# Slot work of three batches joined in the last two head pairs of a chunk-select attention and soft-MoE kernel

## The chip, the core and the metric

The kernel runs on one core of one Trainium2 chip. The metric is device time in microseconds (us), the median of several executions; lower is better. Engines: PE is TensorE, DVE is VectorE, ACT is ScalarE, POOL is GpSimd (it also issues the loads), SP issues the stores.

## The reference, cut to what matters

```python
# attention: B=4, H=8, S=768, D=64; chunks of 32 keys, the 6 best per query by a bound
scores = where(mask(top_chunks, causal), q @ k.T / sqrt(D), -1e9)
x = softmax(scores) @ v                      # -> [3072, 512], all batches in one table
# soft MoE: 8 experts of 4 slots, so 32 slots; F = 1024
logits = x @ phi                             # [3072, 32]
d = softmax of logits down the 3072 rows     # one softmax over all four batches
slot_input = d.T @ x                         # [32, 512]
h = relu(slot_input[e] @ w1[e]);  slot_out[e] = h @ w2[e]
c = softmax of logits along the 32 slots
out = c @ slot_out                           # [3072, 512]
```

The softmax d runs over all rows of all batches, so no slot input is final before the last batch's attention is done.

## The kernel before, in words

The work is cut into 16 pairs of heads, four pairs to a batch (pairs 0 to 3 are batch 0, 12 to 15 batch 3). One hand-written loop (L466 to L550) runs over i from -2 to 15, and iteration i, called pair i here, holds a software pipeline: k and q of pair i + 4 are loaded, k and q of pair i + 2 are transposed on PE and copied by ACT (L181, L190), DVE makes chunk bounds and the split of q (L199 to L216), pair i + 1 gets its chunk selection (ubound, select), pair i gets its scores in six groups (scores, L270 and L280, each group into one of two PSUM buffers) with exponents on ACT (expo, L293) and a causal select on POOL (L295), pair i - 1 gets its product with v (pv, L314, one PSUM buffer), and pair i - 2 is normalised into x (normalise, L326 and L327) and transposed into xT (x_transposes, evac_x). The order in the loop is the order on every engine: each engine takes its instructions strictly as written, and a manual schedule reorders nothing. Matmul results other than scores and pv go through two PSUM buffers (pool p_tp).

The slot work of a batch follows the batch's last pair, two and three iterations later. For batch 0 (last pair 3) it stands in pairs 5 and 6, for batch 1 in pairs 9 and 10, for batch 2 in pairs 13 and 14. At the end of the first of the two, moe_logits (L356, 24 matmuls) and moe_copy (L364 copies the logits, L365 takes each lane's max). In the second, spread over the pair: moe_max (L371 transposes the maxima), moe_bound (L378), moe_exp (a broadcast of the max by PE, the running max m_run, the shifted logits ld, ACT's exponent d_sb at L397 and, from batch 1 on, the rescaling of the sums si_acc), moe_comb (row max L410, difference L412, ACT's exponents into c_pad, L415), moe_dispatch (L426, 30 matmuls that weight x by d and add up the weights, then into si_acc) and moe_ct (L440 transposes c_pad, L443 copies it to cT_all). This is an online softmax: each batch rescales what was summed before. Batch 3 is done behind the loop (L556 to L622), with a few extra matmuls (keep, L570), then come the experts (L650 to L716) and the output (L719 to L745).

The 16 weight blocks (1 MB each in SBUF, w1 of experts 0 to 7, then w2) are loaded by POOL through one software queue, with the loads of k, q and v (192 KB each per pair). Block 0 is issued at the start; the dictionary wplan gives one block to each pair from -1 on except 0 and 1. Blocks 0 to 13 have places of their own (EARLY = 14). Blocks 14 and 15 lie where the input and bound buffers were (pools inp and tpu) and are issued at the start of pairs 14 and 15. The expert code reads blocks 12 to 15 first in experts_out(0, [1], ...), at L711 (the matmul is L694).

Of the kernel before, what the change touches and what calls it, by code (L numbers as in the profile page):

```python
# [46 lines left out]
def kernel(  # L47
# [19 lines left out]
    EARLY = 14  # L67
# [251 lines left out]
    def normalise(i, t0=0, t1=NQT, at=None):  # L319
        b, j = divmod(i, NPB)  # L320
        at = st.pop(("at", i)) if at is None else at
        at = at[:, :, :(t1 - t0) * (D + 1)].rearrange("p h (t d) -> p h t d", t=t1 - t0)
        if j == 0:
            st["x", b] = xp.tile([P, NQT, H, D], BF16, name="x_sb", tag="x_sb")
        inv = tp2.tile([P, 2, NQT, 1], F32, name="inv", tag="inv")[:, :, t0:t1]
        nc.vector.reciprocal(inv, at[:, :, :, D:D + 1])  # L326
        nc.vector.tensor_tensor(  # L327
            st["x", b][:, t0:t1, 2 * j:2 * j + 2, :].rearrange("p t h d -> p h t d"),
            at[:, :, :, :D], inv.broadcast_to([P, 2, t1 - t0, D]), op=ALU.mult,
        )  # L330
# [30 lines left out]
    def moe_copy(b):  # L361
        lg = small.tile([P, NQT, NS], F32, name="lg", tag="lg")
        pm = small.tile([P, NS], F32, name="pm", tag="pm")
        nc.vector.tensor_copy(lg, st.pop(("lgps", b)))  # L364
        nc.vector.tensor_reduce(pm, lg.rearrange("p t s -> p s t"), axis=AX.X, op=ALU.max)  # L365
        st["lg", b], st["pm", b] = lg, pm

    def moe_max(b):
# [2 lines left out]
        nc.tensor.matmul(pmT, lhsT=st.pop(("pm", b)), rhs=identf, is_transpose=True)  # L371
        st["pmT", b] = pmT

    def moe_bound(b):

        pmT = st.pop(("pmT", b))
        mb = small.tile([NS, 1], F32, name="mb", tag="mb")
        nc.vector.tensor_reduce(mb, pmT, axis=AX.X, op=ALU.max)  # L378
        st["mb", b] = mb

    def moe_exp(b):
        lg = st["lg", b]
        bc = p_tp.tile([P, NS], F32, name="bc_ps", tag="tp")
        nc.tensor.matmul(
            bc, lhsT=st.pop(("mb", b)).broadcast_to([NS, P]), rhs=identf[:NS, :NS], start=True, stop=True,
        )
        m_new, m_old = m_run[b % 2], m_run[(b + 1) % 2]
        if b == 0:
            nc.vector.tensor_copy(m_new, bc)
        else:  # L390
            nc.vector.tensor_tensor(m_new, m_old, bc, op=ALU.max)
        ld = small.tile([P, NQT, NS], F32, name="ld", tag="ld")
        nc.vector.tensor_tensor(
            ld, lg, m_new.rearrange("p (o s) -> p o s", o=1).broadcast_to([P, NQT, NS]), op=ALU.subtract,
        )
        d_sb = small.tile([P, NQT, NS], BF16, name="d_sb", tag="d_sb")
        nc.scalar.activation(d_sb, ld, func=ACT.Exp)  # L397
        st["d", b] = d_sb
        if b > 0:

            dm = small.tile([P, 1, NS], F32, name="dm", tag="dm")
            nc.vector.tensor_tensor(dm[:, 0, :], m_old, m_new, op=ALU.subtract)
            nc.scalar.activation(dm, dm, func=ACT.Exp)
            nc.vector.tensor_tensor(si_acc, si_acc, dm.broadcast_to([P, NDG + 1, NS]), op=ALU.mult)

    def moe_comb(b):

        lg = st.pop(("lg", b))
        rm = small.tile([P, NQT, 1], F32, name="rm", tag="rm")
        nc.vector.tensor_reduce(rm, lg, axis=AX.X, op=ALU.max)  # L410
        lc = small.tile([P, NQT, NS], F32, name="lc", tag="lc")
        nc.vector.tensor_tensor(lc, lg, rm.broadcast_to([P, NQT, NS]), op=ALU.subtract)  # L412

        for g in range(2):
            nc.scalar.activation(  # L415
                c_pad[:, :, :, g * SPE:(g + 1) * SPE],
                lc[:, :, g * 16:(g + 1) * 16].rearrange("p t (j s) -> p t j s", j=4), func=ACT.Exp,
            )

    def moe_dispatch(b):  # L420
        d_sb = st.pop(("d", b))
        x = st.pop(("x", b)).rearrange("p t h d -> p t (h d)").rearrange("p t (a c x) -> p t a x c", a=NDG // 2, x=2)
        si = p_tp.tile([P, NDG + 1, NS], F32, name="si_ps", tag="tp")
        for dg in range(NDG + 1):
            for t in range(NQT):
                nc.tensor.matmul(  # L426
                    si[:, dg, :], lhsT=x[:, t, dg // 2, dg % 2, :] if dg < NDG else ones_sq,
                    rhs=d_sb[:, t, :], start=(t == 0), stop=(t == NQT - 1),
                )
        if b == 0:  # L430
            nc.vector.tensor_copy(si_acc, si)
        elif b < B - 1:
            nc.vector.tensor_tensor(si_acc, si_acc, si, op=ALU.add)
        else:
            st["si"] = si

    def moe_ct(b):
        ps = p_tp.tile([P, NQT, P], BF16, name="cT_ps", tag="tp")
        for t in range(NQT):
            nc.tensor.matmul(  # L440
                ps[:, t, :], lhsT=c_pad[:, t].rearrange("p j s -> p (j s)"), rhs=ident, is_transpose=True,
            )
        nc.vector.tensor_copy(cT_all[:, b * NQT:(b + 1) * NQT, :], ps)  # L443
# [12 lines left out]
    for i in (0, 1):
        wplan[i] = 0
    nw = 1

    def weights(i):  # L460
        nonlocal nw
        for _ in range(wplan.get(i, 0)):
            load_w(nw)
            nw += 1

    for i in range(-2, NPAIR):  # L466
        if i >= EARLY:
            wt = ctx.enter_context(tc.tile_pool(name=f"wt{i}", bufs=1))
            w_sb.append(wt.tile([P, NFG * Dm], BF16, name=f"w_sb{i}"))
            weights(i)  # L470
# [5 lines left out]
        moe(moe_max, i - 3)  # L476
# [56 lines left out]
        moe(moe_dispatch, i - 3)  # L533
# [10 lines left out]
        moe(moe_ct, i - 3)  # L544
        moe(moe_logits, i - 2)
        moe(moe_copy, i - 2)
        if i == LAST - 2:
            l_ctx.close()
        if i == LAST - 1:
            u_ctx.close()  # L550

    pads = ctx.enter_context(tc.tile_pool(name="pads", bufs=1))
    siT_pad = pads.tile([P, NDG, E, CH], BF16, name="siT_pad")
    hT_pad = pads.tile([P, NFG, E, CH], BF16, name="hT_pad")
# [52 lines left out]
    st["d", BL] = d_sb  # L607
# [168 lines left out]
```

## Time and profile before

| | us |
|---|---|
| measured time, median of 3 | 173.73 (173.69 to 173.76) |
| span of the profiled execution | 172.0 |
| from one kT copy to the next, pair 8 to 9 | 6.86 |
| pairs 5 to 6, 6 to 7, 7 to 8 | 8.14, 8.75, 7.15 |
| pairs 9 to 10, 10 to 11 | 8.06, 9.56 |
| last exponent of the loop (L293) starts | 134.13 |
| first matmul of the experts (L654) | 141.80 |
| first store issued | 153.58 |

The profiled execution's own time is its span, 172.0 us from the first to the last instruction; the measured time of a run is 1.7 us more. Shares of the span: PE busy 80%, DVE 73%, ACT 71%, POOL 58%. Times in the text are us from the span's start. A line such as L293 is a line of the kernel; a group of instructions is told by its line, engine, and the tiles that it writes and reads.

### The profile page before, as it was taken

What the parts mean: (1) busy time and instruction counts of PE and PEld (TensorE: products, weight loads), DVE (VectorE), ACT (ScalarE), POOL (GpSimd) and SP (SyncE); (2) the same over time, 40 slices, a digit from 0 to 9 for tenths busy, and PEclk for the clock granted to TensorE, in tenths of its full rate; (3) what the DMA queues carried; (4) which work ended last, traced back from release to release, by engine and by line L of the source; (5) the groups of instructions that cost most, each with busy time, mean ns of one, the idle gap of its engine ahead of it and who ended that gap; (6) DMA issues with size and microseconds to landing.
All of it is one profiled execution on the core that took longest, in us unless ns stands there. A gap on an engine that the chain in (4) does not pass through costs nothing.

```text
span 172.0 us, 6181 instructions
## 1 busy us (share of the span) xinstructions
PE 137.7 (80%) x2574; PEld 99.3 (58%) x2575; DVE 126.0 (73%) x429; ACT 122.2 (71%) x163; POOL 99.7 (58%) x192
## 2 busy tenths in 40 slices
PE   0458988999999789999988899999697989896310
PEld 0345465776767658766675676676565854774200
DVE  3468768999999988999997989999843652156530
ACT  2355999999999679899977799998567621265430
POOL 7977759789878666889774678558253710000000
PEclk9999999999999999999999999999999999999955
DMA  3999999999999999999999999999999950019995
GB/s 46 169 145 188 184 213 187 130 159 210 171 203 194 210 198 206 198 205 201 204 202 200 206 197 209 195 211 198 202 210 213 215 107 0 4 37 402 403 406 221
DMA packets 40460, 32.94 MB, mean 191 GB/s; under 512 B 26352, under 2 KB 34544, under 8 KB 40432
## 3 DMA queue, kind: packets, MB, share of 16 engines
q0 software_dynamic: 38416, 26.25, 103.2%
q1 hardware_dynamic: 2016, 6.29, 9.3%
q8 instruction: 20, 0.33, 0.7%
q14 instruction: 8, 0.07, 0.1%
HBM read 52.49 MB, written 6.29 MB: 342 GB/s over the span
## 4 chain that ended last, share of the span: by engine, by line
PE 37%; ACT 27%; DVE 17%; DMA 8%; issue 7%; POOL 0%; ACTq 0%; DVEq 0%; POOLq 0%
ACT e_sb L293 20%; PE sc_ps L270 7%; DMA out_dram<-o_sb 6%; PE tr_ps L181 5%; PE at_ps L314 5%; PE sc_ps L280 4%; DVE x_sb L327 3%; PE h_ps L654 2%; PE so_ps L694 2%; DVE qpn L216 2%; PE ub_ps L229 2%; DMA k_in<-in_k_dram 2%; ACT kT L190 2%; DVE mm L199 2%; DVE mm L205 2%
## 5 line engine op out<-in xcount | busy, mean ns | idle before, releaser
L293 ACT ACTIVATE e_sb<-sc_ps 128x768 bf16<-128x768 f32 (+1 forms) x96 | 82.7, 927 | 7.0 <-PE sc_ps L280 6.5
L295 POOL TENSOR_SCALAR_AFFINE_SELECT e_sb<-e_sb 128x256 bf16<-128x256 bf16 x96 | 39.2, 415 | 25.6 <-ACT e_sb L293 25.3
L270 PE MATMUL sc_ps<-qT,kT 64*128 64x384 bf16 (+3 forms) x288 | 40.2, 297 | 6.6 <-ACT e_sb L293 6.5
L280 PE MATMUL sc_ps<-nsT,smask 64*128 64x384 bf16 (+2 forms) x320 | 38.7, 281 | 0.0
L314 PE MATMUL at_ps<-v_t,e_sb 128*128 128x65 bf16 x672 | 29.8, 194 | 1.8 <-DVE x_sb L327 1.6
L270 PEld LDWEIGHTS <-kT 64*128 64x128 bf16 x288 | 17.3, 95 | 18.3 <-issue 13.2
L314 PEld LDWEIGHTS <-e_sb 128*128 128x128 bf16 x672 | 25.2, 98 | 4.2 <-issue 1.5
L241 DVE MAX8 mx<-ub_ps 128x8 f32<-128x8 f32 (+1 forms) x192 | 17.0, 162 | 3.4 <-POOL e_sb L295 1.9
L280 PEld LDWEIGHTS <-smask 64*128 64x128 bf16 x320 | 16.7, 96 | 3.6 <-issue 0.6
L190 ACT COPY kT<-tr_ps 128x768 bf16<-128x768 bf16 x16 | 12.8, 798 | 8.2 <-PE tr_ps L181 7.1
L199 DVE TENSOR_REDUCE mm<-kT 128x24 bf16<-128x768 bf16 x16 | 15.1, 944 | 4.1 <-ACT kT L190 4.0
L134 POOL DMA_DIRECT2D v_t<-in_v_dram x16 | 16.6, 1041 | 2.0 <-PE ns_ps L252 1.3
L327 DVE TENSOR_TENSOR x_sb<-at_ps,inv 128x768 bf16<-128x768 f32 (+1 forms) x17 | 15.5, 910 | 0.6
L205 DVE TENSOR_REDUCE mm<-kT 128x24 bf16<-128x768 bf16 x16 | 15.1, 943 | 0.0
L190 ACT COPY qT<-tr_ps 128x768 bf16<-128x768 bf16 x16 | 12.9, 805 | 2.1 <-PE tr_ps L181 2.1
L181 PE MATMUL tr_ps<-ident,k_in 128*64 128x128 bf16 x192 | 9.4, 240 | 5.6 <-DMA k_in<-in_k_dram 4.8
L129 POOL DMA_DIRECT2D k_in<-in_k_dram x16 | 11.7, 729 | 1.5 <-POOLq L760 0.8
L740 ACT ACTIVATE o_sb<-o_ps,cinv 128x512 f32<-128x512 f32 x12 | 8.1, 686 | 5.6 <-DMA out_dram<-o_sb 4.3
L129 POOL DMA_DIRECT2D q_in<-in_q_dram x16 | 11.5, 720 | 0.0
L216 DVE TENSOR_SCALAR qpn<-qT 128x768 bf16<-128x768 bf16 x16 | 11.5, 716 | 0.0
L122 POOL DMA_DIRECT2D w_sb<-in_moe_w_dram x16 | 11.3, 708 | 0.0
L738 DVE TENSOR_SCALAR o_sb<-o_ps,cinv 128x512 f32<-128x512 f32 x11 | 8.0, 748 | 4.3 <-DMA out_dram<-o_sb 3.1
(116 smaller groups left out, 195.5 us busy)
## 6 DMA issues: line engine op xcount, KB each, us to landing
w_sb<-in_moe_w_dram POOLq DMA_DIRECT2D x16, 1024.0 KB, 13.4
out_dram<-o_sb SPq DMA_DIRECT2D x10, 512.0 KB, 5.4
k_in<-in_k_dram POOLq DMA_DIRECT2D x16, 192.0 KB, 9.6
q_in<-in_q_dram POOLq DMA_DIRECT2D x16, 192.0 KB, 9.6
v_t<-in_v_dram POOLq DMA_DIRECT2D x16, 192.0 KB, 10.1
out_dram<-o_sb SPq DMA_DIRECT2D x4, 256.0 KB, 3.3
phi_sb<-in_moe_phi_dram POOLq DMA_DIRECT2D x1, 32.0 KB, 8.8
```

Source lines behind the costliest of these rows:

```text
L129: nc.gpsimd.dma_start(out=t, in_=src.rearrange("h (p g) d -> p h (g d)", p=P))
L181: nc.tensor.matmul(ps[h * 64:(h + 1) * 64, g, :], lhsT=src[:, h, g * D:(g + 1) * D], rhs=ident, is_transpose=True,)
L190: nc.scalar.copy(t.rearrange("d (p g) -> d p g", g=NQT), st.pop((nm + "ps", i)).rearrange("d g p -> d p g"),)
L199: nc.vector.tensor_reduce(mm[:, 0, 0, :], kT, axis=AX.X, op=ALU.min)
L205: nc.vector.tensor_reduce(mm[:, 1, 0, :], kT, axis=AX.X, op=ALU.max)
L241: nc.vector.max(mx[:, a, :], ub[:, a, :max(8, 4 * t + 4)])
L270: nc.tensor.matmul(ps[:, h, c:c + w], lhsT=kT[r, kg * P:(kg + 1) * P], rhs=qT[r, qs], start=True, stop=False,)
L280: nc.tensor.matmul(ps[:, h, c + (f - t0) * P:c + (l - t0) * P], lhsT=smask[r, x, kg].rearrange("p a b -> p (a b)"), rhs=nsT[r, (f - x * NJ ...
L293: nc.scalar.activation(e[:, :, :w], st.pop(("scps", i, g))[:, :, :w], func=ACT.Exp, scale=scale)
L295: nc.gpsimd.affine_select(out=e[:, :, :P], in_=e[:, :, :P], compare_op=ALU.is_ge, fill=0.0, base=0, pattern=[[0, 2], [1, P]], channel_mult ...
L314: nc.tensor.matmul(o, lhsT=st["e", i, g][:, h, c:c + P], rhs=v_t[i % NV][:, h, kg, :], start=(kg == 0), stop=(kg == t),)
L327: nc.vector.tensor_tensor(st["x", b][:, t0:t1, 2 * j:2 * j + 2, :].rearrange("p t h d -> p h t d"), at[:, :, :, :D], inv.broadcast_to([P, ...
```

## The change

The logits of batches 0 to 2 are only copied (into lg_all). Their softmax, dispatch and combine weights are done once for all 18 row tiles: the max over all of them at the end of pair 13, its transpose, bound, shift, exponent and the combine exponents spread over pair 14, the transposes for cT and the dispatch (90 matmuls, five sums of 18) over pair 15 and the first lines behind the loop. There is no running max and no rescaling among these batches. For that x of three batches is kept (pool xo, three buffers), c_pad and the logits grow to 18 tiles, and room is made: EARLY is 12, pairs 4 and 8 issue no weight block, pair 12 issues two (blocks 10 and 11), and the blocks 12 to 15 go where buffers have come free: at the end of the loads in pair 13, behind the selection in pair 14, behind the loop, and behind the last use of x, e and the sums in batch 3's part.

```diff
-    EARLY = 14
+    EARLY = 12
+    OLD = B - 1
+    NO = OLD * NQT
...
-    c_pad = static.tile([P, NQT, 4, CH], BF16, name="c_pad")
+    c_pad = static.tile([P, NO, 4, CH], BF16, name="c_pad")
+    lg_all = static.tile([P, OLD, NQT, NS], F32, name="lg_all")
...
     def moe_copy(b):
...
+        nc.vector.tensor_copy(lg_all[:, b], st.pop(("lgps", b)))
+    lgo = lg_all.rearrange("p b t s -> p (b t) s")
+    def old_max():
+        nc.vector.tensor_reduce(pm, lgo.rearrange("p n s -> p s n"), axis=AX.X, op=ALU.max)
+    def old_maxT():
+        nc.tensor.matmul(pmT, lhsT=st.pop("pm"), rhs=identf, is_transpose=True)
+    def old_bound():
+        nc.vector.tensor_reduce(mb, st.pop("pmT"), axis=AX.X, op=ALU.max)
+    def old_shift():
...
+        nc.vector.tensor_copy(m_run, bc)
+        nc.vector.tensor_tensor(
+            ld, lgo, m_run.rearrange("p (o s) -> p o s", o=1).broadcast_to([P, NO, NS]), op=ALU.subtract,
+        )
+    def old_exp():
+        nc.scalar.activation(d_o, st.pop("ld"), func=ACT.Exp)
+    def old_rows():
+        nc.vector.tensor_reduce(rm, lgo, axis=AX.X, op=ALU.max)
+        nc.vector.tensor_tensor(lgo, lgo, rm.broadcast_to([P, NO, NS]), op=ALU.subtract)
+    def old_comb():
+        for g in range(2):
+            nc.scalar.activation(c_pad[:, :, :, g * SPE:(g + 1) * SPE], ..., func=ACT.Exp)
+    def old_dispatch(dgs):
...
+        dispatch(st["si_o"], st["d_o"], [(st["x", b], t) for b in range(OLD) for t in range(NQT)], dgs)
+        if NDG in dgs:
+            nc.vector.tensor_copy(si_acc, st.pop("si_o"))
...
-    wplan = {i: 1 for i in range(-1, NPAIR)}
-    for i in (0, 1):
-        wplan[i] = 0
+    wplan = {i: 1 for i in (-1, 2, 3, 5, 6, 7, 9, 10, 11)}
+    wplan[12] = 2
...
     for i in range(-2, NPAIR):
...
             expo(i, 1)
-        moe(moe_max, i - 3)
+        if i == LAST - 1:
+            old_maxT()
+        if i == LAST:
+            moe_ct(0)
...
             normalise(i - 2)
-        moe(moe_bound, i - 3)
+        if i == LAST - 1:
+            old_bound()
         if have(i + 1):
             select(i + 1)
+        if i == LAST - 1:
+            u_ctx.close()
+            late_weight()
...
             pv(i - 1, [0, 1, 2])
-        moe(moe_exp, i - 3)
+        if i == LAST - 1:
+            old_shift()
+        if i == LAST:
+            old_dispatch([0])
...
             expo(i, 3)
+        if i == LAST - 1:
+            old_exp()
...
-        moe(moe_comb, i - 3)
+        if i == LAST - 1:
+            old_rows()
+        if i == LAST:
+            old_dispatch([1, 2])
...
+        if i == LAST - 2:
+            l_ctx.close()
+            late_weight()
...
             expo(i, 5)
+        if i == LAST - 1:
+            old_comb()
...
-        moe(moe_dispatch, i - 3)
...
-        moe(moe_ct, i - 3)
         moe(moe_logits, i - 2)
         moe(moe_copy, i - 2)
         if i == LAST - 2:
+            old_max()
...
+    t_ctx.close()
+    late_weight()
     BL = B - 1
+    moe_ct(1)
+    old_dispatch([3, 4])
     normalise(LAST - 1)
     pv(LAST, [0, 1, 2])
...
     evac_x(LAST, 3, NQT)
-    keep(2)
+    moe_ct(2, nc.scalar.copy)
     moe_logits(BL, range(NDG - 1, NDG), lg1)
+    i_ctx.close()
+    late_weight()
...
     nc.gpsimd.memset(siT_pad, 0.0)
     nc.gpsimd.memset(hT_pad, 0.0)
```

More of the change, by code (lines that the diff above doesn't have):

```diff
@@ L84 @@
     cT_all = static.tile([P, B * NQT, P], BF16, name="cT_all")
-    c_pad = static.tile([P, NQT, 4, CH], BF16, name="c_pad")
+    c_pad = static.tile([P, NO, 4, CH], BF16, name="c_pad")
+    lg_all = static.tile([P, OLD, NQT, NS], F32, name="lg_all")
     si_acc = static.tile([P, NDG + 1, NS], F32, name="si_acc")
-    m_run = [static.tile([P, NS], F32, name=f"m_run{i}") for i in range(2)]
+    m_run = static.tile([P, NS], F32, name="m_run")
     w_sb = []
@@ L103 @@
     small = ctx.enter_context(tc.tile_pool(name="small", bufs=1))
-    xp = ctx.enter_context(tc.tile_pool(name="xp", bufs=2))
+    xp = ctx.enter_context(tc.tile_pool(name="xp", bufs=1))
     xtp = ctx.enter_context(tc.tile_pool(name="xtp", bufs=1))
-    i_ctx, u_ctx, l_ctx = ExitStack(), ExitStack(), ExitStack()
-    tp3 = i_ctx.enter_context(tc.tile_pool(name="tp3", bufs=3, side="right"))
+    i_ctx, t_ctx, u_ctx, l_ctx = ExitStack(), ExitStack(), ExitStack(), ExitStack()
+    xo = i_ctx.enter_context(tc.tile_pool(name="xo", bufs=OLD, side="right"))
     tp2 = i_ctx.enter_context(tc.tile_pool(name="tp2", bufs=2, side="right"))
@@ L110 @@
     ep3 = i_ctx.enter_context(tc.tile_pool(name="ep3", bufs=5, side="right"))
+    tp3 = t_ctx.enter_context(tc.tile_pool(name="tp3", bufs=3, side="right"))
     tpu = u_ctx.enter_context(tc.tile_pool(name="tpu", bufs=2, side="right"))
@@ L323, in normalise @@
         if j == 0:
-            st["x", b] = xp.tile([P, NQT, H, D], BF16, name="x_sb", tag="x_sb")
+            st["x", b] = (xo if b < OLD else xp).tile([P, NQT, H, D], BF16, name="x_sb", tag="x_sb")
         inv = tp2.tile([P, 2, NQT, 1], F32, name="inv", tag="inv")[:, :, t0:t1]
@@ L361, in moe_copy @@
     def moe_copy(b):
-        lg = small.tile([P, NQT, NS], F32, name="lg", tag="lg")
+        nc.vector.tensor_copy(lg_all[:, b], st.pop(("lgps", b)))
+    lgo = lg_all.rearrange("p b t s -> p (b t) s")
+    def old_max():
         pm = small.tile([P, NS], F32, name="pm", tag="pm")
[L364 to L368, printed above, removed]
+        nc.vector.tensor_reduce(pm, lgo.rearrange("p n s -> p s n"), axis=AX.X, op=ALU.max)
+        st["pm"] = pm
@@ L370, in moe_max @@
+    def old_maxT():
         pmT = p_tp.tile([NS, P], F32, name="pmT_ps", tag="tp")
[L371 to L376, printed above, removed]
+        nc.tensor.matmul(pmT, lhsT=st.pop("pm"), rhs=identf, is_transpose=True)
+        st["pmT"] = pmT
+    def old_bound():
         mb = small.tile([NS, 1], F32, name="mb", tag="mb")
-        nc.vector.tensor_reduce(mb, pmT, axis=AX.X, op=ALU.max)
-        st["mb", b] = mb
@@ L381, in moe_exp @@
-    def moe_exp(b):
-        lg = st["lg", b]
+        nc.vector.tensor_reduce(mb, st.pop("pmT"), axis=AX.X, op=ALU.max)
+        st["mb"] = mb
+    def old_shift():
         bc = p_tp.tile([P, NS], F32, name="bc_ps", tag="tp")
         nc.tensor.matmul(
-            bc, lhsT=st.pop(("mb", b)).broadcast_to([NS, P]), rhs=identf[:NS, :NS], start=True, stop=True,
+            bc, lhsT=st.pop("mb").broadcast_to([NS, P]), rhs=identf[:NS, :NS], start=True, stop=True,
         )
[L387 to L392, printed above, removed]
+        nc.vector.tensor_copy(m_run, bc)
+        ld = small.tile([P, NO, NS], F32, name="ld", tag="ld")
@@ L393, in moe_exp @@
         nc.vector.tensor_tensor(
-            ld, lg, m_new.rearrange("p (o s) -> p o s", o=1).broadcast_to([P, NQT, NS]), op=ALU.subtract,
+            ld, lgo, m_run.rearrange("p (o s) -> p o s", o=1).broadcast_to([P, NO, NS]), op=ALU.subtract,
         )
[L396 to L412, printed above, removed]
+        st["ld"] = ld
+    def old_exp():
+        d_o = small.tile([P, NO, NS], BF16, name="d_o", tag="d_o")
+        nc.scalar.activation(d_o, st.pop("ld"), func=ACT.Exp)
+        st["d_o"] = d_o
@@ L414, in moe_comb @@
+    def old_rows():
+        rm = small.tile([P, NO, 1], F32, name="rm_o", tag="rm_o")
+        nc.vector.tensor_reduce(rm, lgo, axis=AX.X, op=ALU.max)
+        nc.vector.tensor_tensor(lgo, lgo, rm.broadcast_to([P, NO, NS]), op=ALU.subtract)
+    def old_comb():
         for g in range(2):
@@ L416, in moe_comb, with dispatch @@
                 c_pad[:, :, :, g * SPE:(g + 1) * SPE],
-                lc[:, :, g * 16:(g + 1) * 16].rearrange("p t (j s) -> p t j s", j=4), func=ACT.Exp,
+                lgo[:, :, g * 16:(g + 1) * 16].rearrange("p t (j s) -> p t j s", j=4), func=ACT.Exp,
             )
[L420 to L425, printed above, removed]
+    def dispatch(si, d_sb, tiles, dgs):
+        n = len(tiles)
+        for dg in dgs:
+            for k, (x, t) in enumerate(tiles):
+                xt = x.rearrange("p t h d -> p t (h d)").rearrange("p t (a c x) -> p t a x c", a=NDG // 2, x=2)
@@ L426, in moe_dispatch @@
                 nc.tensor.matmul(
-                    si[:, dg, :], lhsT=x[:, t, dg // 2, dg % 2, :] if dg < NDG else ones_sq,
-                    rhs=d_sb[:, t, :], start=(t == 0), stop=(t == NQT - 1),
-                )
[L430 to L437, printed above, removed]
+                    si[:, dg, :], lhsT=xt[:, t, dg // 2, dg % 2, :] if dg < NDG else ones_sq,
@@ L438, in moe_ct @@
+                    rhs=d_sb[:, k, :], start=(k == 0), stop=(k == n - 1),
+                )
+    def old_dispatch(dgs):
+        if 0 in dgs:
+            st["si_o"] = p_tp.tile([P, NDG + 1, NS], F32, name="si_ps", tag="tp")
+        dispatch(st["si_o"], st["d_o"], [(st["x", b], t) for b in range(OLD) for t in range(NQT)], dgs)
+        if NDG in dgs:
+            nc.vector.tensor_copy(si_acc, st.pop("si_o"))
+    def moe_ct(b, copy=nc.vector.tensor_copy):
         ps = p_tp.tile([P, NQT, P], BF16, name="cT_ps", tag="tp")
@@ L439, in moe_ct @@
         for t in range(NQT):
[L440 to L443, printed above, removed]
+            c = c_pad[:, (b % OLD) * NQT + t]
+            nc.tensor.matmul(ps[:, t, :], lhsT=c.rearrange("p j s -> p (j s)"), rhs=ident, is_transpose=True)
+        copy(cT_all[:, b * NQT:(b + 1) * NQT, :], ps)
     def have(i):
@@ L464, in weights, with late_weight @@
             nw += 1
+    def late_weight():
+        n = len(w_sb)
+        wt = ctx.enter_context(tc.tile_pool(name=f"wt{n}", bufs=1))
+        w_sb.append(wt.tile([P, NFG * Dm], BF16, name=f"w_sb{n}"))
+        load_w(n)
     for i in range(-2, NPAIR):
[L467 to L470, printed above, removed]
         if have(i):
@@ L515 @@
             kmax(i + 2)
-        moe(moe_comb, i - 3)
+        if i == LAST - 1:
+            old_rows()
+        if i == LAST:
+            old_dispatch([1, 2])
         if have(i + 2) and i >= 0:
             load_v(i + 2)
-        if i < EARLY:
-            weights(i)
+        weights(i)
+        if i == LAST - 2:
+            l_ctx.close()
+            late_weight()
         if have(i):
@@ L547 @@
         if i == LAST - 2:
[L548 to L554, printed above, removed]
+            old_max()
+    t_ctx.close()
+    late_weight()
     BL = B - 1
+    moe_ct(1)
+    old_dispatch([3, 4])
     normalise(LAST - 1)
@@ L580 @@
     evac_x(LAST, 3, NQT)
-    keep(2)
+    moe_ct(2, nc.scalar.copy)
     moe_logits(BL, range(NDG - 1, NDG), lg1)
+    i_ctx.close()
+    late_weight()
+    pads = ctx.enter_context(tc.tile_pool(name="pads", bufs=1))
+    siT_pad = pads.tile([P, NDG, E, CH], BF16, name="siT_pad")
+    hT_pad = pads.tile([P, NFG, E, CH], BF16, name="hT_pad")
     nc.gpsimd.memset(siT_pad, 0.0)
     nc.gpsimd.memset(hT_pad, 0.0)
-    i_ctx.close()
     tail = ctx.enter_context(tc.tile_pool(name="tail", bufs=1))
-    m_old = m_run[(BL + 1) % 2]
+    m_old = m_run
     pm = small.tile([P, NS], F32, name="pm", tag="pm")
@@ L606 @@
     nc.scalar.activation(d_sb, lg2, func=ACT.Exp)
-    st["d", BL] = d_sb
     rm = small.tile([P, NQT, 1], F32, name="rm", tag="rm")
@@ L617 @@
         nc.scalar.activation(
-            c_pad[:, :, :, g * SPE:(g + 1) * SPE],
+            c_pad[:, :NQT, :, g * SPE:(g + 1) * SPE],
             lc[:, :, g * 16:(g + 1) * 16].rearrange("p t (j s) -> p t j s", j=4), func=ACT.Exp,
@@ L621 @@
     keep(1)
-    moe_dispatch(BL)
+    si = p_tp.tile([P, NDG + 1, NS], F32, name="si_ps", tag="tp")
+    dispatch(si, d_sb, [(st["x", BL], t) for t in range(NQT)], range(NDG + 1))
     op = ctx.enter_context(tc.tile_pool(name="op", bufs=5))
-    si = st.pop("si")
     zrow = tail.tile([1, 4, CH], F32, name="zrow")
```

## The prediction

> **What bounds the kernel now.** I read the page's busy rows first, then the busy times of each engine from one k transpose copy (L190, one per pair up to pair 13) to the next.
>
> ```profile
> span 172.0 us, 6181 instructions
> PE 137.7 (80%) x2574; PEld 99.3 (58%) x2575; DVE 126.0 (73%) x429; ACT 122.2 (71%) x163; POOL 99.7 (58%) x192
> DMA  3999999999999999999999999999999950019995
> ```
> No engine is full over the span, while the DMA row stands at 9 from slice 2 to slice 32: a second thing to watch.
>
> ```profile
> core 0: us, PE busy (x) PEld busy (x) DVE busy (x) ACT busy (x) POOL busy (x), PEclk, DMA share, GB/s
> 51.52:59.66 8.14, 7.20 (x155) 5.56 (x155) 7.70 (x31) 6.58 (x9) 6.36 (x13) 1.00 1.34 202
> 59.66:68.41 8.75, 7.97 (x164) 6.04 (x164) 7.42 (x21) 7.14 (x11) 5.51 (x10) 1.00 1.32 202
> 68.41:75.56 7.15, 6.64 (x130) 4.82 (x130) 6.89 (x28) 6.53 (x10) 5.90 (x12) 1.00 1.37 203
> 75.56:82.42 6.86, 6.54 (x130) 4.72 (x128) 6.46 (x24) 6.52 (x8) 5.84 (x12) 1.00 1.40 201
> 82.42:90.48 8.06, 7.20 (x154) 5.62 (x154) 7.62 (x31) 6.57 (x8) 6.21 (x12) 1.00 1.34 201
> 90.48:100.04 9.56, 8.15 (x168) 6.19 (x168) 7.95 (x28) 7.32 (x12) 5.46 (x11) 1.00 1.29 204
> ```
> These are pairs 5 to 10. A plain pair (8) takes 6.86 us with PE 6.54, ACT 6.52 and DVE 6.46 busy: three engines with 0.3 to 0.4 us to spare, so whatever is added to a pair makes it longer. Pairs 5 to 7 carry batch 0's slot work: 8.14 + 8.75 + 7.15 - 3 x 6.86 = 3.46 us too long. Pairs 9 and 10 carry batch 1's: 8.06 + 9.56 - 2 x 6.86 = 3.90 us. Together 7.36 us.
>
> **Part 1: what leaves batches 0 and 1.** Only the logits and one copy stay in pairs 5 and 9. From the timeline (start, duration) and the groups by line (busy us, mean ns of one, idle before):
>
> ```profile
> 80.89 0.28 PE L270 MATMUL sc_ps<-qT,kT 64*128 64x256 bf16 x2 [0.30 <-ACT e_sb L293]
> 86.87 0.75 PE L356 MATMUL lg_ps<-phi_sb,xT_sb 128*128 128x32 bf16 x24
> 87.55 0.34 PE L270 MATMUL sc_ps<-qT,kT 64*128 64x384 bf16 x2
> ```
> ```profile
> L364 DVE COPY lg<-lg_ps 128x192 f32<-128x192 f32 x3 | 1.0, 339 | 0.0
> ```
> The logits hold PE from 86.87 to 87.55, 0.68 us. A plain pair has a 0.30 us PE wait that takes part of it; 0.38 us stays. The copy's 0.34 us fits into DVE's spare 0.40 us. At worst both lengthen the pair in full, 0.68 + 0.34 = 1.02 us. So this part gains 7.36 - 2 x 0.38 = 6.6 us, at least 7.36 - 2 x 1.02 = 5.3. I take **6.5**.
>
> **Part 2: pairs 14 and 15, in the times of before.** The joint operations work on 576 values a lane where 192 were. Their prices:
>
> ```profile
> 119.50 0.48 DVE L365 TENSOR_REDUCE pm<-lg 128x32 f32<-128x192 f32 x1
> ```
> ```profile
> L199 DVE TENSOR_REDUCE mm<-kT 128x24 bf16<-128x768 bf16 x16 | 15.1, 944 | 4.1 <-ACT kT L190 4.0
> L146 DVE MEMSET c_pad<- 128x384 uint32 x1 | 0.4, 378 | 0.0
> L410 DVE TENSOR_REDUCE rm<-lg 128x6 f32<-128x192 f32 x3 | 1.0, 346 | 0.0
> L397 ACT ACTIVATE d_sb<-ld 128x192 bf16<-128x192 f32 x3 | 1.1, 363 | 4.2 <-DVE ld L393 4.2
> L415 ACT ACTIVATE c_pad<-lc 128x96 bf16<-128x96 f32 x6 | 1.4, 278 | 1.3 <-DVE lc L412 1.3
> L293 ACT ACTIVATE e_sb<-sc_ps 128x1024 bf16<-128x1024 f32 x48 | 47.7, 1028 | 3.9 <-PE sc_ps L280 3.9
> L293 ACT ACTIVATE e_sb<-sc_ps 128x768 bf16<-128x768 f32 x48 | 38.5, 826 | 3.1 <-PE sc_ps L280 2.6 <-POOL e_sb L295 0.4
> ```
> ACT: (1028 - 826)/256 = 0.79 ns a value, so d_o costs 363 + 384 x 0.79 = 0.67 us and each joint c_pad 278 + 192 x 0.79 = 0.43. DVE reductions: from 192 to 768 values 346 becomes 944, 1.04 ns a value with 0.146 us fixed, so the joint row max costs 0.75. The joint max over all tiles reads with a stride, and no trace shows it: between 0.48 (its size costs nothing) and 1.44 (three times L365). I take 0.146 + 3 x 0.334 = 1.15. [...] The memset of c_pad at the start grows threefold, by 0.76 us at most; DVE then waits 4.0 us for the first kT, which hides it.
>
> ```profile
> 120.15 0.96 DVE L327 TENSOR_TENSOR x_sb<-at_ps,inv 128x768 bf16<-128x768 f32 x1
> 121.96 0.39 PE L270 MATMUL sc_ps<-qT,kT 64*128 64x512 bf16 x2
> 123.65 1.92 ACT L293 ACTIVATE e_sb<-sc_ps 128x1024 bf16<-128x1024 f32 x2
> 125.80 1.72 ACT L293 ACTIVATE e_sb<-sc_ps 128x768 bf16<-128x768 f32 x2
> 128.83 1.51 ACT L293 ACTIVATE e_sb<-sc_ps 128x768 bf16<-128x768 f32 x2 [1.30 <-PE sc_ps L280]
> ```
> Pair 14: the joint max puts normalise(12) and the scores of group 2 back by 0.67 us, to 122.6. In return its exponent needn't wait for ld any more (d_o now stands behind group 3): it starts at 123.3, not 123.65. Groups 2 and 3 end at 125.2, d_o at 125.75, groups 4 and 5 at 127.45, the two c_pads (0.8, hidden by nothing) at 128.2. PE has no dispatch here now, so scores 0 and 1 of pair 15 are ready and their exponents start at 128.2, not 128.83: **0.6 gained**. ld, row max and difference (some 0.75 us each) end at 126.2 on DVE, ahead of the c_pads.
>
> ```profile
> 142.84 0.44 PE cT_ps L440 x6
> ```
> ```profile
> 128.33 0.56 DVE L443 COPY cT_all<-cT_ps 128x768 bf16<-128x768 bf16 x1 [0.41 <-PE cT_ps L440]
> 130.08 0.55 PE L314 MATMUL at_ps<-v_t,e_sb 128*128 128x65 bf16 x12 [1.02 <-DVE x_sb L327]
> 140.53 0.75 PE L426 MATMUL si_ps<-d_sb,x_sb 128*128 128x32 bf16 x24
> 141.13 0.30 PE L426 MATMUL si_ps<-d_sb,ones_sq 128*128 128x32 bf16 x6
> ```
> Pair 15: moe_ct(0) holds PE 0.44 us (first row, from the chain of waits; the others are of the timeline). It waits for the c_pads, so its copy starts on DVE at 128.75, and in order behind that copy stands normalise(13), on which pv(14) waits. From copy to pv it was 130.08 - 128.33 = 1.75 us; so pv(14) starts at 130.5, **0.4 late**. Dispatch costs 25 ns a matmul (24 of them from 140.53 to 141.13). So old_dispatch([0]), 18 matmuls, puts scores 2 back by 0.45 and old_dispatch([1, 2]), 36, scores 4 by 0.9: PE is now the engine that ACT waits for. The last exponent of the loop is 0.4 + 1.35 = **1.8 late**.
>
> **Part 3: after the loop.**
>
> ```profile
> 134.02 0.81 PE L314 MATMUL at_ps<-v_t,e_sb 128*128 128x65 bf16 x20
> 134.86 0.51 PE L336 MATMUL xT_ps<-ident,x_sb 128*128 128x128 bf16 x6
> 135.22 0.41 POOL L295 TENSOR_SCALAR_AFFINE_SELECT e_sb<-e_sb 128x256 bf16<-128x256 bf16 x1 [0.78 <-ACT e_sb L293]
> 135.41 0.80 ACT L347 COPY xT_sb<-xT_ps 128x768 bf16<-128x768 bf16 x1 [0.26 <-PE xT_ps L336]
> 136.26 0.60 PE L356 MATMUL lgt_ps<-phi_sb,xT_sb 128*128 128x32 bf16 x18
> ```
> Before, pv(15) started at 134.02 with normalise(14) beside it, xT(14) at 134.86, and the last select ended at 135.63. Now 134.02 + 1.8 = 135.8 is the start of moe_ct(1) (0.44) and old_dispatch([3, 4]) (0.9), to 137.1; the copy into si_acc stands ahead of normalise(14) on DVE, to 137.6; normalise(14) takes 0.25 (the reciprocal) + 0.96, so xT(14) starts at 138.8 and its ACT copy ends at 138.8 + 0.55 + 0.8 = 140.15. The first joint logits of batch 3 follow there, before at 136.26: **3.9 late**. What comes behind keeps its order; moe_ct(2) takes the place of two keep matmuls, and its ACT copy (0.8) lies where ACT waits for the logits of batch 3, and would cost that if it came late.
>
> **Sum.** 3.9 - 6.5 = -2.6 us on the span of 172.0, so 169.4. The measured median, 173.73, lies 1.7 above that span: **171.1 us**.
>
> **The rivals.**
>
> ```profile
> L122 POOL DMA_DIRECT2D w_sb<-in_moe_w_dram x1: 719/719/719, 127.9 to 127.9; - x1
> DMA to landing us min/median/max: 14.4/14.4/14.4
> ```
> ```profile
> 147.90 1.93 PE L694 MATMUL so_ps<-w_sb,hT_pad 128*32 128x256 bf16 x64
> ```
> A, **the last weight block lands late** (slower). Block 15 was issued at 127.9 and landed 14.4 us later, at 142.3; it is first read at 147.90. Now block 14 goes out behind the loop's last select on POOL (135.63 + 1.8 - 6.5, about 131 of the new run) and block 15 behind pv(15) (136.26 + 3.9 - 6.5, about 134), with the memsets of the pads queued behind both, and the first read moves to 147.9 - 2.6 = 145.3. If the queue is as long as it was, it lands at 134 + 14.4 = 148.4, 3.1 us late: span 172.5, 174.2 us. It decides from a landing 11.3 us after the issue. [...] Against it: the queue carries two blocks fewer ahead of k of pair 15 (pairs 4 and 8 issue none), and from 1 MB at the 203 GB/s of the rows above a block takes 5.2 us, two of them some 10.4 from 131, so 142 to 144.
>
> B, **the saving is smaller**: a pair with a weight block moves 1.05 + 0.59 MB, 8.1 us at 203 GB/s, more than 6.87; only pairs 4 and 8 without one keep k and q ahead. If k comes late, or the logits cost 1.02 us, 1 to 2 us of the 6.5 are lost: 172.2 to 173.2.
>
> C, **the deferred work hides better**: with the joint max at its floor (0.67) and no chain of copy, normalise and pv in pair 15 (0.4), 3.9 becomes 2.8; if xT(14) also needn't wait for normalise behind the si_acc copy (PE would be free at 137.1 + 0.8), 2.0: 169.2 to 170.0.
>
> **How the numbers follow.** Forecast 170.0 to 172.2: 0.53. A: 0.17. B: 0.15. C: 0.15. A and the top of B hold what is not faster; 0.2% (0.35 us) is about what a measurement can tell from no change. Faster 0.78, same 0.05, slower 0.17. The range for 8 in 10 runs from 169.2 (C) into A, to 174.2; it leaves out the far end of C and half of A.
>
> **What would show it.** Pairs 5 and 9 at 7.2 to 7.3 us, 6, 7 and 10 at 6.87. In pair 15 a PE wait on x_sb, then ACT waits on scores behind si_ps. Behind the loop xT(14) some 3.9 - 6.5 us from its old place, and no PE wait on a DMA at L694's new line. A wait there is A; pairs of 7.5 us and more, or a PE wait on k_in, are B. Wrong would be above all a loop whose plain pairs change.

## The result, and the profile after

| | before | after |
|---|---|---|
| measured time, median, us | 173.74 (173.69 to 173.76) | 171.21 (170.0 to 173.3) |
| ratio after to before | | 0.983 (95%: 0.981 to 0.986) |
| span of the profiled execution, us | 172.0 | 169.5 |

One execution of the changed kernel, the one of 173.3 us, was disturbed and the ratio leaves it out. A second series gave 171.12 us (e8 below). By that ratio the change makes the kernel 1.7% faster (by the two medians, 1.5%); the forecast was 171.1.

The head of the page of the changed kernel:

```profile
span 169.5 us, 6149 instructions
PE 137.7 (81%) x2567; PEld 98.9 (58%) x2567; DVE 124.0 (73%) x410; ACT 121.8 (72%) x156; POOL 99.8 (59%) x192
...
PEclk9999999999999999999999999999978999999755
DMA  3999999999999999999999999999999799009996
```

The busy times have hardly moved: DVE lost 2.0 us, ACT 0.4, PE nothing. What changed is where the work lies. One new thing is in the clock row, a dip to 7 and 8 three quarters along.

The busy times of each engine from one k transpose copy to the next, pairs 5 to 11 of the changed kernel:

```profile
core 0: us, PE busy (x) PEld busy (x) DVE busy (x) ACT busy (x) POOL busy (x), PEclk, DMA share, GB/s
51.56:58.69 7.13, 7.12 (x158) 5.50 (x158) 6.72 (x26) 6.46 (x9) 5.80 (x11) 1.00 1.61 181
58.69:65.41 6.72, 6.41 (x128) 4.59 (x125) 6.44 (x24) 6.53 (x10) 5.90 (x12) 1.00 1.16 203
65.41:72.28 6.87, 6.55 (x130) 4.73 (x129) 6.46 (x24) 6.53 (x9) 5.85 (x12) 1.00 1.31 195
72.28:79.14 6.86, 6.54 (x129) 4.72 (x128) 6.30 (x24) 6.52 (x8) 5.16 (x11) 1.00 1.38 199
79.14:86.27 7.13, 7.12 (x158) 5.50 (x158) 6.72 (x26) 6.46 (x9) 5.80 (x11) 1.00 1.51 189
86.27:92.99 6.72, 6.36 (x124) 4.47 (x120) 6.62 (x20) 6.53 (x10) 5.74 (x12) 1.00 1.27 205
92.99:100.03 7.04, 6.66 (x130) 4.84 (x131) 6.76 (x27) 6.53 (x9) 5.85 (x12) 1.00 1.36 202
```

Pairs 5 and 9 still hold the logits: PE is busy for 7.12 of 7.13 us. The pair behind each is 0.14 us shorter than a plain one, so a batch leaves 7.13 + 6.72 - 2 x 6.86 = 0.13 us in these two pairs, where 0.38 was forecast. Pair 11 is 0.17 us longer than before (6.87); why was not looked into. The six pairs 5 to 10 take 41.43 us where they took 48.52.

Pair 15 and the stretch behind the loop, PE's timeline (start, duration, in brackets the wait before and who ended it):

```profile
121.23 0.51 PE L437 MATMUL cT_ps<-ident,c_pad 128*128 128x128 bf16 x6 [0.16 <-ACT c_pad L411]
123.52 0.55 PE L318 MATMUL at_ps<-v_t,e_sb 128*128 128x65 bf16 x12 [1.78 <-DVE x_sb L331]
123.91 0.60 PE L421 MATMUL si_ps<-d_o,x_sb 128*128 128x32 bf16 x18
124.45 0.39 PE L274 MATMUL sc_ps<-qT,kT 64*128 64x512 bf16 x2
...
125.65 0.82 PE L340 MATMUL xT_ps<-ident,x_sb 128*128 128x128 bf16 x6
126.26 1.20 PE L318 MATMUL at_ps<-v_t,e_sb 128*128 128x65 bf16 x18
127.27 1.15 PE L421 MATMUL si_ps<-d_o,x_sb 128*128 128x32 bf16 x36
128.36 0.41 PE L274 MATMUL sc_ps<-qT,kT 64*128 64x384 bf16 x2
...
132.85 0.51 PE L340 MATMUL xT_ps<-ident,x_sb 128*128 128x128 bf16 x6 [0.91 <-DVE x_sb L331]
```

DVE's timeline shows what x_sb waited for, the copy of the first c transposes ahead of normalise(13) (L331):

```profile
121.78 0.56 DVE L438 COPY cT_all<-cT_ps 128x768 bf16<-128x768 bf16 x1 [2.10 <-PE cT_ps L437]
122.51 0.96 DVE L331 TENSOR_TENSOR x_sb<-at_ps,inv 128x768 bf16<-128x768 f32 x1
```

DVE stood idle for 2.10 us before that copy, until the transposes of c_pad were done. So the forecast PE wait on x_sb is there (1.78 us), and so are the scores behind si_ps. But from the scores of group 2 (124.45) to those of group 4 (128.36) go 3.91 us, where before 1.99 went, as these rows of the kernel before show:

```profile
130.56 0.39 PE L270 MATMUL sc_ps<-qT,kT 64*128 64x512 bf16 x2
...
132.55 0.34 PE L270 MATMUL sc_ps<-qT,kT 64*128 64x384 bf16 x2
```

The 36 more dispatch matmuls account for 0.9. The rest shows in the durations: the six xT matmuls take 0.82 us, seven microseconds later 0.51. The same kernel's windows of 3.41 us, cut where the granted clock changes:

```profile
121.73:125.14 3.41, 1.63 (x43) 1.37 (x44) 1.65 (x3) 0.89 (x3) 0.81 (x2) 1.00 1.13 213
125.14:128.55 3.41, 3.41 (x68) 2.81 (x64) 0.56 (x1) 1.90 (x2) 0.81 (x2) 0.50 1.06 215
```

In one whole window the granted clock is 0.50, right behind a window in which PE was busy for 1.63 us only. Before, the clock stood at 1.00 from 19.58 to 162.94. ACT pays for it, as its timeline in the changed kernel shows:

```profile
125.10 1.94 ACT L297 ACTIVATE e_sb<-sc_ps 128x1024 bf16<-128x1024 f32 x2 [2.52 <-PE sc_ps L284]
129.03 0.81 ACT L297 ACTIVATE e_sb<-sc_ps 128x768 bf16<-128x768 f32 x1 [2.00 <-PE sc_ps L284]
130.01 1.02 ACT L297 ACTIVATE e_sb<-sc_ps 128x1024 bf16<-128x1024 f32 x1 [0.16 <-PE sc_ps L284]
```

The late blocks 14 and 15, by the loads' line, from 131 to 135:

```profile
L126 POOL DMA_DIRECT2D w_sb<-in_moe_w_dram x2: 713/713/713, 131.6 to 134.5; - x2
...
DMA to landing us min/median/max: 8.2/9.2/10.2
```

Block 15 lands at 134.5 + 10.2 = 144.7; its first read is the group of 64 experts' matmuls at 145.80: 1.1 us to spare, no wait.

### The profile page after: what moved, and what is told of

Same layout as the page of the kernel before. It is cut to its first block, busy times and chain, and to the rows that moved or that the text cites. A ratio compares the mean times of both kernels' runs of the same rounds, so it can differ in the third digit from the quotient of the medians.

```text
span 169.5 us, 6149 instructions
## 1 busy us (share of the span) xinstructions
PE 137.7 (81%) x2567; PEld 98.9 (58%) x2567; DVE 124.0 (73%) x410; ACT 121.8 (72%) x156; POOL 99.8 (59%) x192
## 4 chain that ended last, share of the span: by engine, by line
PE 42%; ACT 25%; DVE 16%; issue 7%; DMA 6%; SPq 0%; DVEq 0%; ACTq 0%; POOLq 0%
ACT e_sb L297 20%; PE sc_ps L274 8%; PE at_ps L318 6%; PE sc_ps L284 5%; PE tr_ps L185 5%; DMA out_dram<-o_sb 4%; DVE x_sb L331 3%; PE ub_ps L233 2%; PE h_ps L669 2%; PE so_ps L709 2%; DMA k_in<-in_k_dram 2%; DVE qpn L220 2%; PE si_ps L421 2%; PE xT_ps L340 2%; DVE mm L203 2%
## 5 line engine op out<-in xcount | busy, mean ns | idle before, releaser
L331 DVE TENSOR_TENSOR x_sb<-at_ps,inv 128x768 bf16<-128x768 f32 (+1 forms) x17 | 15.5, 910 | 0.6
L220 DVE TENSOR_SCALAR qpn<-qT 128x768 bf16<-128x768 bf16 x16 | 12.1, 753 | 0.0
L351 DVE COPY xT_sb<-xT_ps 128x768 bf16<-128x768 bf16 (+1 forms) x15 | 8.0, 536 | 3.8 <-PE xT_ps L340 3.8
```

The lines of the kernel that those rows point to most:

```text
L331: nc.vector.tensor_tensor(st["x", b][:, t0:t1, 2 * j:2 * j + 2, :].rearrange("p t h d -> p h t d"), at[:, :, :, :D], inv.broadcast_to([P, ...
```

## Experiments

All are variants of the changed kernel; times are medians, with the ratio to the kernel before and its 95% interval.

**e1, PE kept busy in its wait**

```diff
         if i == LAST:
             moe_ct(0)
+            st["si_o"] = p_tp.tile([P, NDG + 1, NS], F32, name="si_ps", tag="tp")
+            for _ in range(24):
+                nc.tensor.matmul(st["si_o"].rearrange("p a s -> p (a s)"), lhsT=ident,
+                                 rhs=w_sb[0][:, :(NDG + 1) * NS], start=True, stop=True)
```

> 24 matmuls of no use (128 rows by 160 columns, into the sums' PSUM tile before its real sums start) stand behind the c transposes in pair 15, in PE's 1.78 us wait for x_sb; nothing else is changed. Theory, the granted clock's fall to 0.5 from 125.1 to 128.6 follows from PE's idleness in the 3.4 us before it: the clock stays 1.00 there, scores of group 4 follow scores of group 2 after some 2.9 us instead of 3.9, and the time is 170.0 to 170.2. Rival, those 3.9 us are the dispatch and the crowd of work itself: 3.9 us stay, 171.2.

Measured: 170.62 us, 0.981 (0.977 to 0.985). PE's timeline in e1:

```profile
121.45 1.82 PE L476 MATMUL si_ps<-w_sb,ident 128*128 128x160 bf16 x24
...
124.32 0.39 PE L274 MATMUL sc_ps<-qT,kT 64*128 64x512 bf16 x2
...
127.20 0.34 PE L274 MATMUL sc_ps<-qT,kT 64*128 64x384 bf16 x2
```

Nothing else was moved, the clock stayed at 1.00 from 20.97 to 157.50, and the 3.91 us became 2.88. So the fall costs 1.03 us there. That it follows from PE's idleness is not shown by this one execution: e8 below has the same wait, unfilled, and no fall behind it. The time is 0.59 us lower than the changed kernel's, less than expected, and the two intervals overlap; in the profiled execution block 15 landed at 145.58 and PE waited 0.77 us for it, which takes back most of the 1.24 us by which xT(14) came earlier.

**e2, normalise(13) ahead of the c transposes' copy**

```diff
         if i == LAST:
-            moe_ct(0)
...
         if i == LAST:
+            moe_ct(0)
             old_dispatch([0])
```

> The first c transposes (6 matmuls and their copy on DVE) stand behind the first half of pv(14) in pair 15 instead of ahead of normalise(13). Theory, the chain c_pad, transposes, copy, normalise(13) is what PE waits for ahead of pv(14) and what lets the clock fall: pv(14) starts 1.3 to 2.2 us earlier, no PE wait on x_sb of over 0.6 us there, the clock stays 1.00, and the loop's end is some 2 to 2.8 us earlier; weight block 15 (1.1 us to spare so far) then takes part of it: 168.4 to 169.3. Rival 1, normalise(13) is not what counts and the wait moves to the dispatch: 170.8 to 171.2. Rival 2, only the clock is mended: 170.0 to 170.3.

Measured: 168.49 us, 0.969 (0.966 to 0.973), as expected. PE's timeline in e2:

```profile
121.29 0.55 PE L318 MATMUL at_ps<-v_t,e_sb 128*128 128x65 bf16 x12 [0.22 <-DVE x_sb L331]
...
122.55 0.39 PE L274 MATMUL sc_ps<-qT,kT 64*128 64x512 bf16 x2
...
129.85 0.51 PE L340 MATMUL xT_ps<-ident,x_sb 128*128 128x128 bf16 x6 [0.91 <-DVE x_sb L331]
```

The wait shrinks from 1.78 to 0.22 us, the scores of group 2 come 1.90 us earlier, the clock stays at 1.00 (97.25 to 158.69), and xT(14) is 3.00 us earlier. Six transposes in another place are worth about as much as the whole change brought (2.7 us against 2.5). Both rivals fall. Block 15 landed at 142.59, 0.2 us ahead of its first read.

**e3, weight blocks in every pair again**

```diff
-    wplan = {i: 1 for i in (-1, 2, 3, 5, 6, 7, 9, 10, 11)}
-    wplan[12] = 2
+    wplan = {i: 1 for i in (-1, 2, 3, 4, 5, 6, 7, 8, 9, 10, 11)}
```

> Pairs 4 and 8 issue a weight block again and pair 12 one instead of two (the same blocks, the same total). Theory, the load queue has no room in the shortened pairs (a pair with a block moves 1.64 MB, some 8 us at 203 GB/s, against 6.87): k of the later pairs lands late, PE waits on k_in, 1 to 4 us longer: 172.2 to 175. Rival, the loads have slack of several us as before the change: 171.2.

Measured: 176.37 us, 1.012 (1.007 to 1.016): slower than the kernel before, and above the range expected. PE's waits in e3 (us in total, times, longest):

```profile
PE tr_ps L185 <- DMA k_in<-in_k_dram: 10.2, 6, 4.8
```

In the changed kernel this row is 4.8 us, once, at the start. The five new waits of 5.4 us together are 5.2 us of time. Rival B's mechanism is real: pairs of 6.87 us leave the queue no room for a block each, and skipping pairs 4 and 8 keeps the gain (e6 and e9 skip them too, with the spare block in another place).

**e4, 1 MB more ahead of block 14**

```diff
     t_ctx.close()
+    load_w(11)
     late_weight()
```

> Block 11 is loaded a second time, right ahead of the late load of block 14: 1 MB more in the queue. Theory, block 15 had 1.1 us to spare at its first read, and 1 MB takes some 5 us: PE waits on a DMA at the experts' second matmul group and the time grows by 3.5 to 4.5 us: 174.7 to 175.7. Rival, the blocks land side by side and the queue has room: under 1 us more, 171.2 to 172.2.

Measured: 177.99 us, 1.019 (1.014 to 1.025). PE's waits in e4:

```profile
PE so_ps L710 <- DMA w_sb<-in_moe_w_dram: 4.0, 1, 4.0
```

The loads do not land side by side: block 15 landed at 148.87 instead of 144.71, though it was issued 1.15 us earlier (133.38 against 134.53), and PE waited 3.97 us. That is rival A, at the place it named. The time grew by more than expected, in the profiled execution (span 173.9) by 4.4 us and in the others by up to 7. Behind the idle wait the clock fell to 0.50 for a window of the experts' matmuls (149.45 to 152.86) in the profiled execution; the others had a lower mean clock still (0.94 to 0.95, it 0.96).

**e5, normalise(14) first behind the loop (on e2)**

```diff
+    normalise(LAST - 1)
     moe_ct(1)
     old_dispatch([3, 4])
-    normalise(LAST - 1)
```

> e2_norm_first (168.49, the first c transposes behind the first half of pv(14)) with, behind the loop, normalise(14) ahead of the transposes for cT of batch 1 and of dispatch [3, 4], so that on DVE it no longer stands behind the copy into si_acc. Theory, that copy and the order on DVE hold xT(14) back by the 0.91 us that PE waits there: xT(14) starts some 0.9 us earlier. The end follows only in part, since in e2 block 15 landed 4.94 us behind block 14 (the queue runs without a gap) and 0.2 us ahead of its first read: PE then waits some 0.6 us on the DMA at the experts' matmuls, 168.2 to 168.4. Rival, block 15 lands as much earlier as it is issued: no such wait, 167.6. Rival, PE itself is the limit there: xT(14) unchanged, 168.5.

Measured: 168.32 us (167.74 to 169.97), 0.970 (0.966 to 0.974). A row of PE's timeline in e5 and, behind it, one of its waits:

```profile
128.95 0.50 PE L340 MATMUL xT_ps<-ident,x_sb 128*128 128x128 bf16 x6
```
```profile
PE so_ps L708 <- DMA w_sb<-in_moe_w_dram: 2.4, 1, 2.4
```

xT(14) comes 0.90 us earlier, as expected, and its wait is gone. In this execution, the slowest of the six, the gain is lost to block 15; only this one has a trace. The blocks ran some 2 us later than in e2 (block 12 landed at 129.77, there at 127.90), so the loads' pace differs between executions by more than the room that is left (0.2 us in e2).

**e6, a block earlier (on e5)**

```diff
-    wplan = {i: 1 for i in (-1, 2, 3, 5, 6, 7, 9, 10, 11)}
-    wplan[12] = 2
+    wplan = {i: 1 for i in (-1, 0, 2, 3, 5, 6, 7, 9, 10, 11, 12)}
```

> e5_norm14 with the second block of pair 12 issued in pair 0 instead, where the queue runs nearly empty (k lands 4.2 us after its issue in pair 1). Theory, the late blocks are held by the queue alone: block 15 lands 2 to 4 us ahead of its first read, no PE wait on a DMA there, 167.4 to 167.7. Rival, the extra block makes k of pairs 5 to 8 late (PE waits on k_in): 168.5 or more.

Measured: 168.27 us, 0.969 (0.964 to 0.973): no gain. Block 13 landed 3.6 us earlier than in e2 (129.13 against 132.76), but block 15 at 142.59, where it landed in e2. So it was not the queue ahead that held it: two blocks issued at 128.86 and 130.91, when nothing else was left in the queue from 129.13 on, land 7.8 and 11.7 us later. The theory fails; what fits is that the issue counts, and so the place that comes free late. The rival did not come either: PE waits on k_in once, at the start.

**e7, the tail's pieces in place of the extra matmuls (on e6)**

```diff
     normalise(LAST - 1)
-    moe_ct(1)
-    old_dispatch([3, 4])
+    old_dispatch([3])
...
-    keep(2)
+    old_dispatch([4])
...
-    keep(1)
+    moe_ct(1, nc.scalar.copy)
```

> e6_early_block with two pieces of the tail put where matmuls of no use kept PE busy in batch 3's softmax: dispatch [4] (18 matmuls, 0.45 us) in place of keep(2), the transposes for cT of batch 1 (0.35 us) in place of keep(1), with their copy on ACT. Theory, behind the loop PE is the limit up to xT(14) once normalise(14) isn't: xT(14) starts 0.5 to 0.8 us earlier than in e6, the end follows: 166.7 to 167.2. Rival, normalise(14) on DVE is still the later one: under 0.3 us, 167.4.

Measured: 171.19 us, 0.982 (0.980 to 0.985), 2.9 us worse than e6. PE's timeline and a window of e7:

```profile
132.39 0.49 PE L437 MATMUL cT_ps<-ident,c_pad 128*128 128x128 bf16 x6 [0.45 <-DVE xT_sb L351]
...
133.78 0.22 PE L605 MATMUL pmT_ps<-identf,m_run 1*32 1x1 f32 x2 [0.60 <-ACT cT_all L438]
```
```profile
135.00:141.83 6.83, 6.46 (x82) 3.62 (x84) 2.12 (x10) 1.70 (x5) 0.00 (x0) 0.50 0.89 178
```

xT(14) gained 0.3 us (the rival: DVE is the later one), and two new waits cost 1.05: the sums hold one of the two PSUM buffers longer, and the rest goes through the other, copy by copy. Then the clock fell for two windows. How the 2.9 us divide between the waits and the clock is not separated.

**e8, e9, e10: what the clock costs in the time.** e8 is the changed kernel again; e9 is it with e6's wplan; e10 is e1 with e6's wplan.

> The changed kernel as it is, again, beside the next two. 171.2, with single runs near 170.0 where the clock stays 1.00 in pair 15 and near 171.2 where it falls.

> The changed kernel with only the second weight block of pair 12 issued in pair 0 instead. Theory, in the changed kernel the queue is not what the end waits for: no gain, 171.0 to 171.3, with the clock at 0.5 for 3.41 us in pair 15 as before. Rival, block 15 is what limits many of the runs: 170.3 to 170.7.

> e1_warm (24 matmuls of no use in PE's wait for x_sb) with the block of pair 0 as in e9_early_only, so that block 15 is not held by the queue. Theory, the fall of the clock costs 1.0 to 1.2 us and in e1_warm block 15 took half of the gain: 169.9 to 170.2, no PE wait on a DMA at the experts of over 0.3 us. Rival, the clock's fall costs nothing at the end: as e9_early_only.

Measured: e8 171.12 us, 0.982 (0.977 to 0.987); e9 171.40, 0.983 (0.978 to 0.988); e10 170.41, 0.979 (0.974 to 0.984). e8 was expected to have single executions near 170.0 and had none. e9 gained nothing, so the queue was not the changed kernel's limit. e10 is 0.99 us below e9, the size expected, though above its range of 169.9 to 170.2; PE waited for no weight block. But the intervals overlap, so the price of the fall in the measured time is supported and not separated. It also fits that of the changed kernel's executions in both series, the one of 173.3 us apart, one at a mean clock of 0.974 took 170.0 us and six at 0.959 to 0.964 took 170.95 to 171.29. The windows of e8, cut at its clock's changes:

```profile
112.63:116.04 3.41, 2.01 (x40) 1.62 (x38) 3.34 (x16) 1.51 (x2) 1.34 (x4) 1.00 1.06 214
116.04:119.45 3.41, 3.41 (x32) 2.02 (x33) 2.37 (x8) 2.47 (x3) 1.76 (x4) 0.50 1.10 209
122.87:126.28 3.41, 1.78 (x44) 1.37 (x44) 1.54 (x3) 0.89 (x2) 0.81 (x2) 1.00 1.06 214
126.28:129.69 3.41, 3.41 (x88) 2.73 (x84) 0.56 (x1) 2.52 (x3) 0.82 (x2) 1.00 1.06 214
```

PE's timeline in e8, pair 15:

```profile
124.50 0.55 PE L318 MATMUL at_ps<-v_t,e_sb 128*128 128x65 bf16 x12 [1.78 <-DVE x_sb L331]
...
125.43 0.39 PE L274 MATMUL sc_ps<-qT,kT 64*128 64x512 bf16 x2
...
128.31 0.34 PE L274 MATMUL sc_ps<-qT,kT 64*128 64x384 bf16 x2
```

Here the fall came in pair 14, behind the joint max, where PE waits too (1.1 us at L378), and not in pair 15: the same kernel with the same wait of 1.78 us, and 2.88 us from the scores of group 2 to those of group 4. e4, which is the changed kernel up to there, shows 2.88 us too. That is the price of the fall, 1.03 us, without any edit. But it is also the rival that e1 leaves standing: where the windows begin varies from run to run (the first rise is at 19.33 in the changed kernel, at 20.47 in e8), and that alone may be why the wait passed without a fall. Of the five profiled executions with the wait unfilled, three show a fall in pair 15 (the changed kernel from 125.14, e3 from 130.56, e9 from 124.33) and two none (e4, e8); of the two with it filled (e1, e10), none. In e10's, too, the fall came in pair 14 (0.50 from 116.75 to 120.16). So the change made two stretches in which the clock can fall; that filling the wait prevents the fall is supported, not shown.

**e11, blocks 12 to 15 read later (on e6)**

```diff
-    experts_out(0, [1], [0, 1])
-    experts_out(1, [0, 1], [0])
+    experts_out(1, [0], [0, 1])
+    experts_out(0, [1], [0])
+    experts_out(1, [1], [0])
     nc.scalar.activation(so_sb[0], so_ps[0], func=ACT.Copy, scale=zinv)
-    experts_out(1, [0, 1], [1])
+    experts_out(0, [1], [1])
+    experts_out(1, [1], [1])
```

> e6_early_block with the experts' second products in another order: those of experts 0 to 3 for both halves of F first, so that blocks 12 to 15 are read 0.9 us later. Theory, block 15 is what limits e2, e5 and e6: no PE wait on it is left and the time is 167.5 to 168.0. Rival, the wait for the second half of hT_pad takes its place (PE goes there 0.9 us sooner): 168.3 or more.

Measured: 167.35 us (167.29 to 168.25), 0.962 (0.957 to 0.966), the fastest version, 3.8% below the kernel before. Among PE's waits there is none on w_sb, and the group of 64 follows without one:

```profile
141.91 1.93 PE L707 MATMUL so_ps<-w_sb,hT_pad 128*32 128x256 bf16 x64
```

So block 15 limited e6, and e5 before it, as far as the times tell: e11 is 0.9 us below e6, of which it differs by the reading order alone, but e6's profiled execution waited only 0.18 us for the block and the two intervals overlap a little. The rival's wait for hT_pad did not come.

## Why the prediction was right, point by point

The time was right to 0.1 us; the steps were right in kind. That it was so close is luck: three sizes were off, by 0.65 us, 1.2 us and 0.5 us, and cancelled.

- **Part 1, "6.5"**: too small. The k transpose copy of pair 13 moved from 113.77 to 106.90, 6.87 us, and the first exponents of pair 14 from 119.77 to 112.62, 7.15. The mis-sized term is the logits' 0.38 us a batch, which measured 0.13: 0.27 in their own pair, of which the pair behind gives back 0.14. Pair 11 lost 0.17 again. The last 0.28 us, in pair 13, I had not looked for.
- **Part 2, the operations**: right. Joint max 1.13 us (1.15), d_o 0.69 (0.67), both c_pads 0.80 (0.8), row max 0.74 (0.75).
- **Pair 15's start**: 0.63 us gained, forecast 0.6.
- **The chain of copy, normalise and pv in pair 15**: the right mechanism; pv(14) came 7.15 - 6.56 = 0.59 us late, forecast 0.4. But it was called a delay of 0.4 us, in rival C too, and not seen as the place to mend. e2 shows that the order is worth 2.7 us, and the fall of the clock behind the wait is part of that.
- **"The last exponent is 1.8 late"**: 3.0 in these terms (from 134.13, less 7.15, to 130.01). The step that failed is that dispatch was the only thing added to PE there, at 25 ns a matmul: the sum has no term for the clock. 1.03 of the 1.2 us missing is the clock that fell to 0.50 (the changed kernel against e8, the same kernel without the fall there, and against e1), the rest the pv above.
- **Behind the loop, 3.9 - 1.8 = 2.1 more**: exact. From the last exponent (4.12 us earlier) to xT(14) (132.85, 2.01 earlier) 2.1 us were lost; of these the 0.91 us of normalise(14) behind the copies of cT and of the sums is shown by e5.
- **The end**: xT(14) 2.0 us earlier, the first store (153.58 to 151.47) 2.1, the last landing (171.02 to 168.51) 2.5. The last 0.4 us came from the stores: from first issue to last landing 17.04 us instead of 17.44, and 17.0 to 17.1 in the variants. No step spoke of it, and its cause was not tried.
- **Sum**: 7.15 gained, 5.1 lost, 0.5 gained behind it: 2.5, where the forecast was 6.5 - 3.9 = 2.6.
- **The rivals**: A did not happen, but was 1.1 us away; e4 makes it happen. Its landing was forecast as 142 to 144 and was 144.7. B did not happen because two pairs skip their block (e3); its 172.2 to 173.2 is 0.1 more than 171.1 plus 1 to 2 us. C's premise, that the chain in pair 15 can be had for nothing, is what e2 makes true, and its 168.49 us lies below C's 169.2.

## What to carry to other kernels

Before deferred work is priced by its own durations, look at what each moved instruction waits for and what it stands ahead of on its engine: here a copy of 0.56 us that nothing needed soon, and that itself waited 2.10 us for its input, stood ahead of the normalise on which PE and then ACT hung. When a kernel's pairs become shorter than their loads take, as here, the loads' plan has to be thinned at once, or the queue takes the gain back (e3, 176.37 us against 171.21). And a fix moves the bound: after each, look at which wait ends last now, since a second fix (e5, e6) may give nothing until a third (e11) is made.

## What was not expected of the hardware

The granted clock fell to 0.50 for whole windows of 3.41 us, on a grid that starts with the clock's first rise (in the changed kernel's timeline twelve k transposes take 0.85 us at 16.39 and 0.53 at 23.52): in the changed kernel at 125.14 = 19.33 + 31 x 3.413, in e8 at 116.04 = 20.47 + 28 x 3.413, where 3.413 us is the length of the changed kernel's fall, 125.14 to 128.55. The windows ahead of the falls inside the work had PE busy for 1.31 us (e9), 1.63 (changed kernel, e3), 2.01 (e8), 2.03 (e10) and 2.34 (e7); only e4's, behind the wait for block 15, was nearly idle (0.54). In all of these but e4 PE was busy for 0.38 (1.31 of 3.41 us) to 0.69 (2.34) of the window. Busy time alone does not decide: e8's window from 122.87 had 1.78 us and no fall came. What decides stays open.
